# Block-sparse attention into a top-2 mixture of experts: a mask write moved ahead of the row maximum, the last batch's router logits moved behind an expert's second tile, scatters of one unit left unordered, and an exponential moved

## The chip, the cores and the metric

The kernel runs on one core of a Trainium2 chip. The metric is device time in microseconds (us), the median of the runs shown. TensorE (PE) multiplies matrices; VectorE (DVE), ScalarE (ACT) and GpSimd (POOL) do the other arithmetic; SyncE (SP) only issues DMAs. Each engine runs its own instructions in the order in which the program wrote them, and waits on semaphores for the others.

## The reference

Two parts, one behind the other. The attention, for 4 batches, 8 heads, 768 positions and a head size of 64:

```
scores = scale * q @ k.T                      # scale = 1/8
mask   = blocks of 32: neighbours, the first and last block, 3 sampled ones
scores = where(mask, scores, -1e9);  attn = exp(scores - max);  attn /= sum + 1e-9
out    = attn @ v
```

Its output, as x of 3072 tokens by 512, goes into eight experts:

```
noisy  = x @ w_gate + log1p(exp(x @ w_noise)) * noise
top2   = the two largest of 8;  top2_w = exp(top2_l - max) / (sum + 1e-9)
out[token] += top2_w * (relu(x[token] @ w1[e]) @ w2[e])     # 512 -> 1024 -> 512
```

## The kernel before, in words

**Attention** takes the first 380 us. A head has 6 tiles of 128 keys, so there are 192 steps. A step n computes exponentials of one tile of scores (`exp`, lines 290 to 304: PE writes `pe`, ACT writes `p`, in two halves), turns the 32-bit result into 16-bit pairs on DVE (`halve`, line 309), and multiplies the tile of three steps earlier with the values (`av`, line 335, 18 small matmuls into `po`). A head later in the program has its row maxima found meanwhile (`max_mm`, lines 251 and 252 on PE into `pm`, line 254 on ACT into `rl`; `max_red`, line 261 on DVE). When the six maxima of a head are there, `row_mm` (line 281) turns them into rows on PE, beside the `pm` of that step, and `row_put` (line 288, DVE) writes them into rows of `q2`, from which the exponentials subtract them. At the end of a head `av_end(.., "copy")` (line 347, ACT) copies `po` into `xo`, after which `po` may take the next head; DVE and POOL scale it. `Attention.steps` writes all this in one fixed order, and calls `background` between, which runs the router.

**Router.** `Router.run` is a generator, one for each batch of 768 tokens, and each `yield` is a place where it may pause. For the first three batches it runs in the gaps of the attention. For the last batch it pauses only at `MARK`, and `to_mark` (called from the expert loop) runs it to the next. It computes logits on PE (lines 586 and 588, from `r_xT`, the transposed tokens), copies them (line 595, `r_lc`), finds the two largest, computes the slot of each token (lines 677 to 717), and POOL scatters the token numbers and weights into the table `slots` in 12 indirect DMAs (line 723).

**Experts.** There are nine units. Unit 0 is expert 0 with 640 rows of the first three batches, unit 1 is expert 0's remaining 224 rows, units 2 to 8 are experts 1 to 7 with 816 rows. A unit has eight tiles of the first layer (`mm1`, line 892 on PE, line 897 on ACT and 898 on DVE: `hh` and `hl`, the high and low part) and up to seven chunks of 128 rows of the second layer (`mm2`, line 912). `finish` weights a chunk (line 940, DVE, `y`) and POOL scatters it into the output (line 942). Before that, POOL gathers what earlier units left there (line 858, `pv`). Weights arrive in 8 pieces an expert (line 797, SP) and are split into a high part (line 804, ACT) and a low part (line 805, DVE). Unit 0 starts while the last batch has yet to be routed. Unit 1 needs that routing: the slots, then the list `mt` (lines 814 and 818), the indices `gi` (line 827), the token rows `xg` (line 843, POOL) and their transpose `xtb` (line 853).

Of the kernel before, what the change touches and what calls it, by code (L numbers as in the profile page):

```python
# [44 lines left out]
class Attention:  # L45
# [271 lines left out]
    def later(self, steps, f):  # L317
        if steps:
            self.todo.setdefault(self.now + steps, []).append(f)
        else:  # L320
            f()
# [113 lines left out]
    def steps(self, on_group, background):  # L435
        NSTEP, LM, LA, GT = self.NSTEP, self.LM, self.LA, self.G * self.T
        for n in range(NSTEP + LA + 6 + self.ROWLATE):
            g, i = divmod(n, GT)
            self.now = n
            for f in self.todo.pop(n, []):  # L440
                f()
            for at, nm in self.LOADAT:
                if i == at and 4 <= g + 3 < self.NG:
                    self.load(g + 3, None, nm)
            for f, *a in self.plan.pop(n, []):
                f(*a)
            new = range(self.nmax, min(n + self.lead(n) + 1, self.T + self.XM + 1 + (n + 1) * self.RN // 4, NSTEP))
            self.nmax = max(self.nmax, new.stop)
            j = n - LA
            last = 0 <= j < NSTEP and j % self.T == self.T - 1  # L450
            if last:
                self.av(j)
            if n < NSTEP:
                self.exp(n, 0)
            self.av_end(j, "copy", on_group)
            slow = 1 if j < NSTEP - GT else 0
            self.av_end(j - 3 - slow, "high", on_group)
            if j == NSTEP - GT:
                self.av_end(j - 4, "high", on_group)
            self.age()  # L460
            for m in new:
                self.max_mm(m)
            self.row_mm()
            if n < NSTEP:
                self.exp(n, 1)
            if 0 <= j < NSTEP and not last:
                self.av(j)
            background(n, 0)
            self.av_end(j - 1, "sum", on_group)
            for m in new:  # L470
                self.max_red(m)
            if n < NSTEP:
                self.halve(n)
            self.row_put()
            background(n, 1)
            self.av_end(j - 1, "inverse", on_group)
            background(n, 2)
            self.av_end(j - 1, "scale", on_group)
            self.av_end(j - 4 - slow, "low", on_group)
            if j == NSTEP - GT:  # L480
                self.av_end(j - 5, "low", on_group)
            for at, part in self.VSPLITAT:
                if i == at and 2 < g + 2 < self.NG:
                    self.vsplit(g + 2, part)
            if i == self.DIFFAT and g + 2 < self.NG:
                self.diff(g + 2, slice(0, self.G))
            for at, part, h in self.CASTAT:
                if i == at and g + 3 < self.NG:
                    self.split(g + 3, part, h)
            for at, part in self.SPLITAT:  # L490
                if i == at and 0 < g < self.NG - 2:
                    self.split(g + 2, part)
            for at, part, h in self.FIRST:
                if g == 0 and i == at:
                    self.split(2, part, h)
            background(n, 3)


class Router:
# [73 lines left out]
    def run(self, b, ps):  # L573

        nc, T, D, pool = self.nc, self.T, self.D, self.pool
        KB = D // P
        last = b == self.B - 1
# [11 lines left out]
                                 stop=kb == KB - 1, skip_group_check=True)  # L589
        for _ in range(0 if last else self.HO):  # L590
            yield
        if last:
            yield self.MARK
        lc = tile([P, T, 32], F32, "lc")
        nc.vector.tensor_copy(lc, pv)
        yield
# [8 lines left out]
        u = tile([P, T, E], F32, "u")  # L605
# [51 lines left out]
        nc.vector.tensor_scalar(z0, ef, 0.0, None, op0=ALU.is_equal)  # L657
        yield
        yield self.MARK if last else None
        ex = tile([P, T], F32, "ex")  # L660
        nc.scalar.activation(ex, dl, AF.Exp)
        for _ in range(0 if last else self.YN):
            yield
        if last:
            yield self.MARK

        pp = ps()
        po = pp[:, 0:T * E].rearrange("p (t e) -> p t e", t=T)
# [51 lines left out]
        for t in range(T):  # L720
            for k in range(2):
                nc.gpsimd.memset(self.spacer, 0.0)
                s = nc.gpsimd.indirect_dma_start(
                    out=self.table, out_offset=bass.IndirectOffsetOnAxis(ap=sl[:, t, k:k + 1], axis=0),
                    in_=pi[:, t, k, :], in_offset=None)
# [7 lines left out]
class Experts:  # L733
# [200 lines left out]
    def finish(self, u, c, py):  # L934

        nc = self.nc
        r = self.st["u", u]
        m = self.rows_of(u, c)
        y = self.yp.tile([P, self.D], F32, name="y")
        nc.vector.scalar_tensor_tensor(y[0:m], py[0:m, 0:self.D], r["mt"].bitcast(F32)[0:m, c, 1:2], self.pv[0:m, c, :],  # L940
                                       op0=ALU.mult, op1=ALU.add)
        nc.gpsimd.indirect_dma_start(  # L942
            out=self.out, out_offset=bass.IndirectOffsetOnAxis(ap=r["mt"][0:m, c, 0:1], axis=0),
            in_=y[0:m], in_offset=None, bounds_check=self.N - 1, oob_is_err=False)


def overflow(tc, router, w1, w2, out, x_dram, table):
# [78 lines left out]
def kernel(ctx, tc, q, k, v, sampled_blocks, w_gate, w_noise, noise, w1, w2, out):  # L1026
    nc = tc.nc
# [8 lines left out]
    ex = Experts(tc, router, w1, w2, out, x_dram, table)  # L1036
# [18 lines left out]
    def to_mark():  # L1055
        while jobs:
            m = next(jobs[0], jobs)
            if m is jobs:
                jobs.pop(0)
            elif m == Router.MARK:  # L1060
                return
# [65 lines left out]
    for u in range(nu):  # L1127
# [5 lines left out]
        nn = nf + bool(nl)  # L1133
        for f in range(ex.FB):
            ex.mm1(u, f)
            to_mark()
            if u > 1 and f == 0 and nn:
                ex.meta(u + 1)
            if u == 0:
                for i in SPLITS[f]:  # L1140
                    ex.split_piece(0, i)
                    if i + 3 < 8:
                        ex.load_piece(0, i + 3)
            if u == 0 and f in (5, 6):

                ex.load_piece(1, f - 5)
            if u > 1 and nn and f >= 5:
                ex.load_piece(nxt, f - 5)
            if u == 2 and f == 0:
                ex.split_piece(e, 6)  # L1150
            if u > 1 and f == 1:
                ex.split_piece(e, 7)
            if u > 1 and f == 1 and nn:
                ex.indices(u + 1)
            if u > 1 and f < n:
                ex.paced(ex.gather_prev(u, ex.chunks(u)[f]))
            if u > 1 and 1 <= f <= nn:
                ex.paced(ex.gather(u + 1, f - 1))
            if u > 1 and 2 <= f <= nn:
                ex.xpose(u + 1, f - 2)  # L1160
# [59 lines left out]
```

## Time and profile before

| what | value |
|---|---|
| median of 3 runs | 954.87 us (949.98, 957.19, 954.87) |
| profiled execution | 961.59 us, of which the span is 959.8 us |
| mean granted clock of PE | 0.985 |
| busy: PE, DVE, ACT, POOL | 876.8, 526.2, 447.9, 353.2 us |
| attention, router of the first three batches | to about 382 us |
| unit 0 with the last batch's routing | 382 to 449.6 us |
| units 1 to 8 | 449.6 to 943 us |
| last scatter, overflow count | to 959.8 us |

The span is one execution on the core, and the 1.8 us between it and the time of that execution lie around it. The profiled execution is 6.7 us over the median. A window of the span says how long each engine was busy in it and at what granted clock, and a line of a timeline says what an instruction waited for ahead of it.

### The profile page before, as it was taken

The page shows a single profiled execution, that of the slowest core. Times are in us where ns is not written, and L with a number is a line of the kernel's source. Part 1 is how long each engine was busy: PE and PEld are TensorE (multiplying, and loading weights), DVE is VectorE, ACT ScalarE, POOL GpSimd, SP SyncE. Part 2 cuts the span into 40 slices and gives each one's busy share as a digit, 9 for nine tenths or more (in the row PEclk, how much of TensorE's full clock was granted, in tenths as well). Part 3 has the DMA queues.
Part 4 walks back from the last instruction along what each step waited for, and adds up shares of the span by engine and source line. Part 5 has one row for each costly group of instructions (what it writes and reads, how often), then busy time and mean ns, then how long its engine had stood idle before and what let it go on. Part 6 is the DMA issues. An engine that isn't in the chain of part 4 may idle for free.

```text
span 959.8 us, 21119 instructions
## 1 busy us (share of the span) xinstructions
PE 876.8 (91%) x8494; PEld 529.3 (55%) x8494; DVE 526.2 (55%) x1245; ACT 447.9 (47%) x973; POOL 353.2 (37%) x392
## 2 busy tenths in 40 slices
PE   6899998898899878798999999999999999999993
PEld 3566675566566546554655554554554554555541
DVE  7888889898989966452334323333333333333210
ACT  6989988898888755331322122222231231231200
POOL 5432232662364163265252342332432432523220
PEclk9999999999999989899999999999999999999997
DMA  7677776796779249548788296295493692782110
GB/s 206 140 180 191 189 155 155 155 183 171 155 161 177 57 80 181 157 79 205 192 184 211 92 225 174 73 230 165 113 246 111 142 235 91 180 211 83 55 43 29
DMA packets 206477, 145.56 MB, mean 152 GB/s; under 512 B 142182, under 2 KB 183271, under 8 KB 206370
## 3 DMA queue, kind: packets, MB, share of 16 engines
q1 hardware_dynamic: 173936, 80.07, 40.0%
q0 software_dynamic: 14256, 39.58, 13.7%
q10 hardware_dynamic: 18178, 24.48, 9.9%
q8 instruction: 68, 1.11, 0.5%
q14 instruction: 39, 0.32, 0.1%
HBM read 79.55 MB, written 26.32 MB: 110 GB/s over the span
## 4 chain that ended last, share of the span: by engine, by line
PE 47%; DMA 3%; issue 1%; POOL 1%; DVE 1%; SPq 0%; ACT 0%; POOLq 0%; ACTq 0%
PE ph L892 23%; PE py L912 22%; PE py L921 2%; DMA pv<-out_dram,gi 1%; DMA out_dram<-y,mt 1%; DMA xg<-x_rows,gi 1%; DVE y L940 1%; DMA xtb<-xg 1%; POOL xg L843 1%; DMA slots<-r_pay,r_sl 0%; DMA mt<-slots 0%; POOL pv L858 0%; SPq L853 0%; POOL out_dram L942 0%; DVE hl L898 0%
## 5 line engine op out<-in xcount | busy, mean ns | idle before, releaser
L304 ACT ACTIVATE p<-pe 128x384 int32<-128x384 f32 x384 | 193.3, 530 | 44.6 <-PE pe L303 25.7
L897 ACT ACTIVATE hh<-ph 128x408 f16<-128x408 f32 (+2 forms) x136 | 66.8, 492 | 269.8 <-PE ph L892 209.7
L898 DVE SCALAR_TENSOR_TENSOR hl<-ph,hh 128x408 f16<-128x408 f32 (+2 forms) x136 | 76.0, 560 | 172.7 <-ACT hh L897 159.6
L942 POOL DMA_INDIRECT out_dram<-y,mt x56 | 74.9, 1337 | 216.3 <-DVE y L940 105.2
L335 PEld LDWEIGHTS <-p 128*128 128x128 f16 x3456 | 127.4, 98 | 24.4 <-issue 1.7
L301 PE MATMUL pe<-q,k 128*128 128x384 f16 x384 | 127.2, 331 | 10.3 <-ACT p L304 5.4
L309 DVE TENSOR_SCALAR p<-p 128x1536 f16<-128x1536 uint16 x192 | 125.9, 656 | 7.4 <-ACT p L304 7.0
L303 PE MATMUL pe<-q,k 102*128 102x384 f16 x384 | 127.2, 331 | 0.9 <-DVE q L288 0.9
L912 PEld LDWEIGHTS <-hh 128*128 128x128 f16 x768 | 74.8, 98 | 95.5 <-issue 9.9
L261 DVE CUSTOM_DVE_ANT_0 rl<-pm,rl 128x384 f32<-128x384 f32 x192 | 106.1, 554 | 36.9 <-ACT rl L254 27.5
L335 PE MATMUL po<-vb,p 128*128 128x65 f16 x1152 | 122.2, 194 | 0.7 <-issue 0.7
L335 PE MATMUL po<-vx,p 128*128 128x65 f16 x1152 | 122.3, 195 | 0.5 <-DVE p L309 0.4
L940 DVE SCALAR_TENSOR_TENSOR y<-py,mt,pv 128x512 f32<-128x512 f32 (+2 forms) x56 | 41.2, 748 | 147.5 <-PE py L912 140.8
L335 PE MATMUL po<-vl,p 128*128 128x64 f16 x1152 | 122.0, 193 | 0.0
L892 PE MATMUL ph<-xta,w1hb 128*128 128x408 f16 x512 | 109.3, 336 | 0.0
L254 ACT ACTIVATE rl<-pm 128x384 f32<-128x384 f32 x192 | 100.2, 523 | 14.3 <-PE pm L252 13.2
L251 PE MATMUL pm<-k,q 88*128 88x384 f16 x192 | 65.4, 341 | 30.2 <-DVE q L288 21.6
L892 PE MATMUL ph<-xtb,w1ha 128*128 128x408 f16 (+1 forms) x448 | 91.2, 325 | 0.5 <-DMA xtb<-xg 0.5
L858 POOL DMA_INDIRECT pv<-out_dram,gi x56 | 56.8, 1014 | 94.2 <-ACT hh L897 65.6
L912 PE MATMUL py<-w2ha,hh 128*128 128x512 f16 x192 | 73.3, 382 | 4.6 <-DVE y L940 4.6
L892 PEld LDWEIGHTS <-w1ha 128*128 128x128 f16 x576 | 56.5, 99 | 36.0 <-DMA xtb<-xg 1.0
L224 POOL TENSOR_TENSOR kn<-raw_k,kn 128x384 f16<-128x384 f32 (+1 forms) x29 | 28.8, 993 | 124.8 <-ACT kn L222 103.6
(200 smaller groups left out, 1625.2 us busy)
## 6 DMA issues: line engine op xcount, KB each, us to landing
wraw<-in_moe_w_dram SPq DMA_DIRECT2D x60, 512.0 KB
raw_v<-in_v_dram ACTq DMA_DIRECT2D x16, 384.0 KB
out_dram<-zero ACTq DMA_DIRECT2D x24, 256.0 KB
x_rows<-x SPq DMA_DIRECT2D x16, 384.0 KB
raw_k<-in_k_dram ACTq DMA_DIRECT2D x12, 384.0 KB
raw_q<-in_q_dram ACTq DMA_DIRECT2D x12, 384.0 KB
k<-k SPq DMA_DIRECT2D x15, 192.0 KB
q<-q SPq DMA_DIRECT2D x15, 192.0 KB
```

The lines of the kernel that those rows point to most:

```text
L254: self.nc.scalar.activation(rl, pm[:, 1, 0:384], AF.Relu)
L261: self.nc.vector.tensor_tensor_reduce(rl, pm[:, 0, 0:384], rl, 1.0 / 64.0, -3.0e38, ALU.add, ALU.max, accum_out=mn[:, self.MR + t:self.MR ...
L301: nc.tensor.matmul(pe[:, 0:384], r["k1"][:, h, c, :], r["q1"][:, h, t, :], start=True, stop=False)
L303: nc.tensor.matmul(pe[:, 0:384], r["k2"][0:K, h, c, :], r["q2"][0:K, h, t, :], start=False, stop=True)
L304: nc.scalar.activation(p32[:, t].rearrange("p t c -> p (t c)"), pe[:, 0:384], AF.Exp, scale=0.125)
L309: self.nc.vector.tensor_scalar(p.rearrange("p t c w -> p (t c w)"), p32.bitcast(U16).rearrange("p t c -> p (t c)"), HC, None, op0=ALU.mult)
L335: self.nc.tensor.matmul(o, p[:, t, :, w], v, start=first and i == 0, stop=last and i == 2, skip_group_check=True)
L892: nc.tensor.matmul(ph[:, b, 0:m], w[wt][:, kb, fs], r["xt"][:, kb, a, o:o + m], start=i == 0, stop=i == last)
L897: self.pace = nc.scalar.activation(hv, ph[:, b, 0:m], AF.Relu)
L898: nc.vector.scalar_tensor_tensor(self.hl[:, f, o:o + m], ph[:, b, 0:m], 0.0, hv, op0=ALU.max, op1=ALU.subtract)
L912: nc.tensor.matmul(py, h[:, f, o], w[x][:, f, :], start=i == 0, stop=i == last)
L942: nc.gpsimd.indirect_dma_start(out=self.out, out_offset=bass.IndirectOffsetOnAxis(ap=r["mt"][0:m, c, 0:1], axis=0), in_=y[0:m], in_offset= ...
```

## The change

Five edits, of which the last touches two places.

1. In `Attention.steps`, `row_put` stands ahead of `max_red` and `halve` of its step, no longer behind them.
2. In the same function `av_end(j, "copy")` stands behind `max_mm` and `row_mm`, no longer ahead of them.
3. In `Router.run`, the last batch does not pause between its logits and their copy. For the other batches the exponential of the gates (line 661) stands behind the pauses and not ahead of them.
4. In the expert loop the last batch's router is not run behind the first tile of the first layer, only behind the second and later ones, and there behind the split and load of the weight pieces.
5. The scatters of one unit into the output are declared independent of each other, since a token has one slot of an expert. The gathers of the next unit wait for all of them.

```diff
@@ Attention.steps
             if n < NSTEP:
                 self.exp(n, 0)
-            self.av_end(j, "copy", on_group)
...
             for m in new:
                 self.max_mm(m)
             self.row_mm()
+            self.av_end(j, "copy", on_group)
...
             self.av_end(j - 1, "sum", on_group)
+            self.row_put()
             for m in new:
                 self.max_red(m)
             if n < NSTEP:
                 self.halve(n)
-            self.row_put()
@@ Router.run
         for _ in range(0 if last else self.HO):
             yield
-        if last:
-            yield self.MARK
         lc = tile([P, T, 32], F32, "lc")
...
         yield self.MARK if last else None
+        for _ in range(0 if last else self.YN):
+            yield
         ex = tile([P, T], F32, "ex")
         nc.scalar.activation(ex, dl, AF.Exp)
-        for _ in range(0 if last else self.YN):
-            yield
-        if last:
-            yield self.MARK
+        yield self.MARK if last else None
@@ Experts.finish
-        nc.gpsimd.indirect_dma_start(
+        s = nc.gpsimd.indirect_dma_start(
             out=self.out, ...
+        done = r.setdefault("done", [])
+        for p in done:
+            self.tc.declare_no_dep(s.ins, p.ins, reason="a token has one slot of an expert")
+        done.append(s)
@@ the expert loop
             ex.mm1(u, f)
-            to_mark()
-            if u > 1 and f == 0 and nn:
-                ex.meta(u + 1)
             if u == 0:
                 for i in SPLITS[f]:
                     ex.split_piece(0, i)
                     if i + 3 < 8:
                         ex.load_piece(0, i + 3)
+            if f:
+                to_mark()
+            if u > 1 and f == 0 and nn:
+                ex.meta(u + 1)
```

DVE at the end of a head, before:

```order
L261 ISA rl,mn_107<-pm,rl 128x384 [waits Activation_49]
L261 ISA mn_107 128x1
L309 TENSOR_SCALAR p_931<-p_914 128x1536 [waits Activation_49]
L350 TENSOR_SCALAR rc<-xo 128x6
L261 ISA rl,mn_107<-pm,rl 128x384 [waits DVE_49,Activation_49]
L261 ISA mn_107 128x1
L309 TENSOR_SCALAR p_972<-p_935 128x1536 [waits Activation_49]
L288 TENSOR_TENSOR q_101<-pm,ident 6x768
L352 RECIPROCAL rc<-rc 128x6 [waits DVE_49]
```

and now:

```order
L261 ISA rl,mn_107<-pm,rl 128x384 [waits Activation_49]
L261 ISA mn_107 128x1
L309 TENSOR_SCALAR p_931<-p_914 128x1536 [waits Activation_49]
L350 TENSOR_SCALAR rc<-xo 128x6
L288 TENSOR_TENSOR q_101<-pm,ident 6x768 [waits Activation_49]
L261 ISA rl,mn_107<-pm,rl 128x384 [waits DVE_49]
L261 ISA mn_107 128x1
L309 TENSOR_SCALAR p_973<-p_935 128x1536 [waits Activation_49]
L352 RECIPROCAL rc<-rc 128x6 [waits DVE_49]
```

The write of the mask rows (line 288) passes one reduction and one halving, and takes over the reduction's wait for ACT.

ACT at the same place, before:

```order
L304 ACTIVATE p_914<-pe 128x384 [waits DVE_49,PE_49]
L347 ACTIVATE xo<-po 128x390
L254 ACTIVATE rl<-pm 128x384 [waits PE_49]
L304 ACTIVATE p_914<-pe 128x384 [waits PE_49]
L304 ACTIVATE p_935<-pe 128x384 [waits DVE_49,PE_49]
```

and now:

```order
L304 ACTIVATE p_914<-pe 128x384 [waits DVE_49,PE_49]
L254 ACTIVATE rl<-pm 128x384 [waits PE_49]
L347 ACTIVATE xo<-po 128x390
L304 ACTIVATE p_914<-pe 128x384 [waits PE_49]
L304 ACTIVATE p_935<-pe 128x384 [waits DVE_49,PE_49]
```

The copy that frees `po` stands behind the `rl` of the first of the two steps; nothing else moved.

DVE in unit 0, where the last batch's logits are copied, before:

```order
L805 SCALAR_TENSOR_TENSOR w1la<-wraw,w1ha 128x4x256 [waits DMAHW2_49,Activation_49]
L805 SCALAR_TENSOR_TENSOR w1la<-wraw,w1ha 128x4x256 [waits DMAHW5_49,Activation_49]
L898 SCALAR_TENSOR_TENSOR hl<-ph,hh 128x320 [waits Activation_49] x2
L595 COPY r_lc<-py 128x192
L598 TENSOR_TENSOR r_lg<-r_lc 128x96 [waits DVE_49]
```

and now (the line numbers of the changed kernel are 2 or 3 lower):

```order
L802 SCALAR_TENSOR_TENSOR w1la<-wraw,w1ha 128x4x256 [waits DMAHW2_49,Activation_49]
L802 SCALAR_TENSOR_TENSOR w1la<-wraw,w1ha 128x4x256 [waits DMAHW5_49,Activation_49]
L895 SCALAR_TENSOR_TENSOR hl<-ph,hh 128x320 [waits Activation_49] x2
L802 SCALAR_TENSOR_TENSOR w1la<-wraw,w1ha 128x4x256 [waits DMAHW7_49,Activation_49]
L593 COPY r_lc<-py 128x192 [waits PE_49]
L596 TENSOR_TENSOR r_lg<-r_lc 128x96 [waits DVE_49]
```

On DVE the third split (of piece 3) stands ahead of the copy; on PE all 24 matmuls of a second tile stand ahead of the logits.

POOL, the last scatter of the slots, the first two scatters of unit 0's output and the first gather of unit 1's rows, before:

```order
L723 DMA slots<-r_pay,r_sl 28160x2 [waits DMASW1_49]
L942 DMA out_dram<-y,mt 3072x512 [waits DMAHW5_49,DMASW2_49,DVE_49]
L942 DMA out_dram<-y,mt 3072x512 [waits DMASW3_49,DMASW2_49,DVE_49]
L843 DMA xg<-x_rows,gi 128x1024 [waits DMAHW0_49,DMAHW6_49,DMASW4_49,DVE_49]
L843 DMA xg<-x_rows,gi 96x1024 [waits DMAHW1_49,DMASW5_49,DVE_49]
```

and now:

```order
L720 DMA slots<-r_pay,r_sl 28160x2 [waits DMASW1_49]
L939 DMA out_dram<-y,mt 3072x512 [waits DMAHW5_49,DMASW2_49,DVE_49]
L939 DMA out_dram<-y,mt 3072x512 [waits DMASW3_49,DVE_49]
L840 DMA xg<-x_rows,gi 128x1024 [waits DMAHW0_49,DMAHW6_49,DMASW4_49,DVE_49]
L840 DMA xg<-x_rows,gi 96x1024 [waits DMAHW1_49,DMASW5_49,DVE_49]
```

The second scatter no longer waits for DMASW2, the semaphore that the first one raises; the order of the rows is the same.

## Rows read from the trace of the kernel before

**Rows 1.** Windows: length; PE, PEld, DVE, ACT, POOL busy; clock, DMA share, GB/s.

```profile
37.00:315.00 278.00, 248.94 (x3836) 177.00 (x3833) 250.07 (x688) 242.50 (x595) 109.49 (x132) 1.00 0.76 169
384.00:408.00 24.00, 18.52 (x167) 13.04 (x166) 11.55 (x45) 7.86 (x16) 6.92 (x7) 0.86 0.53 157
```

**Rows 2.** Waits of PE, 37 to 315 us: us in total, times, longest.

```profile
PE pm L251 <- DVE q L288: 20.4, 22, 2.0
```

**Rows 3.** Waits of ACT, the same stretch.

```profile
ACT p L304 <- PE pe L303: 18.5, 30, 2.1
```

**Rows 4.** Timeline, DVE at one head's end: start, us, engine, line, idle before.

```profile
103.45 0.56 DVE L261 CUSTOM_DVE_ANT_0 rl<-pm,rl 128x384 f32<-128x384 f32 x1 [0.86 <-ACT rl L254]
104.59 0.56 DVE L261 CUSTOM_DVE_ANT_0 rl<-pm,rl 128x384 f32<-128x384 f32 x1
105.07 0.55 DVE L309 TENSOR_SCALAR p<-p 128x1536 f16<-128x1536 uint16 x1
105.66 0.96 DVE L288 TENSOR_TENSOR q<-pm,ident 6x768 f16<-6x768 f32 x1
```

**Rows 5.** Timeline, ACT at that head's end and one gap behind it.

```profile
102.50 0.54 ACT L347 ACTIVATE xo<-po 128x390 f32<-128x390 f32 x1
102.87 0.55 ACT L254 ACTIVATE rl<-pm 128x384 f32<-128x384 f32 x1
103.98 0.57 ACT L254 ACTIVATE rl<-pm 128x384 f32<-128x384 f32 x1
112.03 0.49 ACT L304 ACTIVATE p<-pe 128x384 int32<-128x384 f32 x1 [0.38 <-PE pe L303]
```

**Rows 6.** Timeline, PE at that head's end.

```profile
103.09 0.19 PE L335 MATMUL po<-vx,p 128*128 128x65 f16 x1
106.68 0.34 PE L251 MATMUL pm<-k,q 88*128 88x384 f16 x1 [0.81 <-DVE q L288]
```

**Rows 7.** Timeline, POOL products at this head and a later one.

```profile
105.48 0.91 POOL L224 TENSOR_TENSOR qn<-raw_q,qn 128x384 f16<-128x384 f32 x1 [2.12 <-ACT qn L222]
147.96 0.91 POOL L224 TENSOR_TENSOR qn<-raw_q,qn 128x384 f16<-128x384 f32 x1 [2.16 <-ACT qn L222]
```

**Rows 8.** Timeline, DVE at that later head.

```profile
148.04 1.25 DVE L309 TENSOR_SCALAR p<-p 128x1536 f16<-128x1536 uint16 x1
```

**Rows 9.** Timeline, PE in units 0 and 1.

```profile
390.50 0.21 PE L586 MATMUL py<-r_whl,r_xT 128*128 128x32 f16 x1 [4.87 <-DMA r_xT<-x]
442.14 0.38 PE L912 MATMUL py<-w2ha,hh 128*128 128x512 f16 x1 [3.41 <-DVE y L940]
449.63 0.37 PE L892 MATMUL ph<-xtb,w1ha 128*128 128x224 f16 x2 [0.46 <-DMA xtb<-xg]
```

**Rows 10.** Timeline, DVE in unit 0.

```profile
387.99 2.36 DVE L805 SCALAR_TENSOR_TENSOR w1la<-wraw,w1ha 128x1024 f16<-128x1024 f32 x2 [0.45 <-ACT w1ha L804]
398.67 0.35 DVE L595 COPY r_lc<-py 128x192 f32<-128x192 f32 x1
403.91 1.22 DVE L805 SCALAR_TENSOR_TENSOR w1la<-wraw,w1ha 128x1024 f16<-128x1024 f32 x1
409.61 0.24 DVE L677 TENSOR_TENSOR r_A<-r_A,py 128x96 f32<-128x96 f32 x1
440.20 1.23 DVE L805 SCALAR_TENSOR_TENSOR w1lb<-wraw,w1hb 128x1024 f16<-128x1024 f32 x1 [2.90 <-issue]
```

**Rows 11.** Timeline, POOL: first slot scatter, second scatter of the output.

```profile
411.80 1.02 POOL L723 DMA_INDIRECT slots<-r_pay,r_sl  x1 [19.02 <-DVE r_ot L715]
434.97 0.99 POOL L942 DMA_INDIRECT out_dram<-y,mt  x1 [4.42 <-DMA mt<-slots]
```

**Rows 12.** Chain of waits, two pieces ahead of unit 1: start, us, what.

```profile
432.75 2.19 DMA mt<-slots
...
436.27 6.36 DMA xg<-x_rows,gi
```

**Rows 13.** Timeline, ACT: the gates' exponential of the third batch.

```profile
324.80 0.21 ACT L661 ACTIVATE r_ex<-r_dl 128x6 f32<-128x6 f32 x1 [2.68 <-DVE r_dl L639]
```

## The prediction

> **What bounds the kernel now.** I read the stretches first (windows), then each engine's waits in the attention, then one head row by row, then the chain of waits and the timelines between 384 and 450 us. The windows show that the attention from 37 to 315 us has no single bound: of 278.0 us PE is busy 248.94, DVE 250.07 and ACT 242.50 [rows 1]. Three engines at 87 to 90% mean that small stalls pass from one to the next. PE's largest stall there is a matmul of a later head's maxima (line 251) that waits for the mask write on DVE (line 288): 20.4 us in 22 waits, 0.93 each [rows 2]. ACT's largest is for PE's scores: 18.5 us in 30 waits [rows 3]. These are largely the same stalls, seen one engine further on, so they must not be added.
>
> The second place is unit 0. PE waits 4.87 us for the transposed tokens [rows 9] and the clock of that stretch falls to 0.86 [rows 1]. The route to unit 1 then runs: logits copied at 398.67, slots multiplied out at 409.61 [rows 10], first slot scatter at 411.80 [rows 11], lists in `mt` [rows 12], rows gathered [rows 12], transposed, and unit 1's first matmul at 449.63, which waits a last 0.46 us for them [rows 9]. What is gained on that route, PE gains whole, since everything behind it is PE work.
>
> **Attention, edits 1 and 2.** In one head, DVE does reduction (103.45), halving, sum, reduction (104.59), halving (105.07), mask write (105.66 to 106.62), and PE's matmul starts at 106.68 [rows 4, 6]. With the write ahead, it still waits for the second `rl`, which ACT ends at 104.55 (103.98 + 0.57) [rows 5]. So it can run from about 104.58 to 105.54. The buffer `pm` is also read by the reduction of that step, which now follows, 0.56 long [rows 4]: free at about 106.13 where it was 106.62, so 0.5 us of the 0.81 wait goes [rows 6]. The halving ends about 1 us later; its values are multiplied three steps on, and a step takes 1.9 us (192 steps from 24 to 382 us), so there is cover.
>
> ACT's copy of `po` starts 0.37 later, one pitch of ACT (102.50 to 102.87 [rows 5]). PE's first `av` of the next head came at 103.09, when the copy had ended at 103.04 [rows 5, 6], so it now waits some 0.3 us. I find so little slack (0.05 us) in 14 of 31 heads, 0.3 to 0.9 in the others. That delay falls ahead of the wait for the mask write and eats what is left of it, so the two don't add: the head's stall goes from 0.93 to 0.3 or 0.4.
>
> What is this worth? PE's view gives 0.5 x 22 = 11 us, ACT's gives its gap behind a stall, 0.38 [rows 5], x 22 = 8.4. ACT is as busy as PE, so I take the smaller, rounded to **8 us**. The bounds: nothing, if other waits take the place; and 20.4, the whole wait [rows 2].
>
> **The exponential of the gates, edit 3.** ACT stands 2.68 us at 324.80 for DVE's `r_dl` [rows 13]. Two steps later its input is ready. But DVE is busy all through that stretch with the router and remains so; what ACT gains, it then waits for DVE. I take 0.4 us, one gap of ACT as in [rows 5]; bounds 0 and 2.7. The other two batches show no such wait, so nothing.
>
> **Logits behind the second tile, edits 3 and 4.** PE has the 3.3 us of the second tile as cover for the 4.87 of waiting [rows 9]; tokens still land at 390.50, so the logits end at about 391.6 as before. What delayed the copy was not this: DVE had `hl` of the second tile in front of the copy at 398.67 [rows 10]. Now the second tile is over by 388.6. DVE finishes the double split at 387.99 + 2.36 = 390.35 [rows 10], the two `hl` parts at 391.8, waits for ACT's high part of piece 3 until 392.3, splits its low part (1.22 [rows 10]) and copies the logits at about 393.5: 5.2 us earlier. Behind the router's first part stand the same two tiles and two splits as before (pieces 4 and 5 for 3 and 4), 5.7 us from there to the multiplication. With ACT's order a little less favourable I get 404.85 for 409.61, **4.8 us** earlier. The 12 slot scatters, their landing and `mt` keep their lengths, so `mt` and the loads on SP behind it move by 4.8.
>
> **Free scatters, edit 5.** The second scatter, issued at 434.97 [rows 11], had its `y` ready at 429.15 and waited for the first scatter's landing; the gathers of unit 1 stood behind it on POOL until 436.27 [rows 12]. Now they wait for `gi` alone, computed when `mt` lands (432.75 + 2.19 = 434.94 for its last part [rows 12], the first index at 434.41). That takes another 1.3 to 1.6 from the gathers, so the transposed rows come 6.3 earlier. PE can't use all of it: its last chunk of unit 0 starts at 442.14, having waited for a `y` [rows 9], which stood on DVE behind the split at 440.20, whose piece SP loads behind `mt` [rows 10]. That moves by 4.8. The chunk then runs 7.0 us to 449.17, and the 0.46 behind it disappears [rows 9]. Unit 1 starts 4.8 + 0.46 = **5.2 us** earlier. Bounds: 2, if a load or scatter queues anew, and 6.3. Later units wait for `y` or nothing, not for scatters; there I count 0, hidden by the 24 us units of PE work.
>
> PE's clock: it fell to half behind the 4.87 us wait (0.86 over the stretch [rows 1]). The wait now is 390.50 - 388.6 = 1.9 us, and may leave the clock up. The route is paced by DVE here, so I count nothing for it either way.
>
> **Sum.** 8 + 0.4 + 5.2 = 13.6 us. The profiled execution would go from 961.6 to 948.0; it stands 6.7 over the median. From the median 954.9 I predict **941.3 us**.
>
> **A rule that speaks against it.** The halving now stands later, where POOL works. At 148.04 a halving took 1.25 us where it takes 0.55 elsewhere [rows 4, 8], with a POOL product of 0.91 begun 0.08 us before it [rows 7]. In the head above, the product starts at 105.48, behind the halving at 105.07 [rows 4, 7]; now the halving would come at about 106.1 and meet it. In 14 heads such a product starts within 0.35 us of the mask write. The price is 0.3 to 0.7 us each on DVE, 4 to 10 us in all, which takes half of the attention's gain or all of it: 945 to 950. The Trainium skill states in "SBUF — State Buffer" (Who interferes with whom) that VectorE and GpSimd share a port pair as an exclusive lock, and that whichever starts second blocks for the other's whole instruction. The trace agrees in the one row of 1.25 us; by that rule alone the time would be in the band just named.
>
> **Rivals.**
> - *The attention gains nothing.* Either the halving meets POOL as said, or ACT, 87% busy, sets the pace. For it: three engines are near their limit [rows 1]. Against: the stall is in 22 heads and ACT's gap follows it [rows 2, 5]. Time 954.9 - 5.6 = 949.3.
> - *The whole wait goes.* If the buffer is not what PE waits for but the written rows, the result is there 1.1 us earlier and nearly all of 20.4 us can go on PE [rows 2]; with ACT following, 15 to 20 us. Time 931.
> - *Slower: the copy behind the `rl`.* PE can't start a head's `av` before `po` is copied; ACT's queue is full at this place, so each of 31 heads loses 0.37 us [rows 5], 11.5 us, and if nothing is gained on the mask write (the stall there is set by ACT's second `rl`), this decides. With 5.2 back in unit 0: 954.9 + 11.5 - 5.2 = 961.2. It decides if PE's first `av` waits for the copy in most heads and the write's wait stays over 0.8. Against: the slack in over half of the heads.
> - *Unit 0 gains only 2.* A new wait on DVE or for a piece of weights: 944.5, within the range.
>
> **Chances.** Forecast (with the last rival) 0.55, attention nothing 0.26, whole wait 0.12, slower 0.07. About 1% is what a measurement of this kernel can tell from no change: under 945.3 is faster, over 964.4 slower. Of the forecast 0.46 lies under 945.3, with the 0.12 that is 0.58 faster. The slower rival's 961 lies mostly within 1%: 0.02 of its chance is over. Same: 0.38 and slower 0.04. The range from 932 to 951 leaves out half of the 931 case and the slow one and the edges.
>
> **What the profile after would show.** Right: the waits of line 251 on the mask write fall from 20.4 to under 10, the wait of ACT for scores to about 10; the attention ends near 374 instead of 382. The logits' copy about 5 us closer behind unit 0's start, the first slot scatter 25 us behind it and not 30, the second output scatter without a wait for the first; unit 1 62 us behind unit 0's start, not 67.5. Wrong: a new wait of `av` for the copy of `po` on ACT, halvings over 1 us beside each mask write, or a `mt` that moves while PE's last chunk does not.

## The result, and the profile after

The changed kernel takes 946.66 us (median of 16 runs, 941.88 to 952.45), the kernel before 954.88 us (16 runs, 949.98 to 963.27) on the same chip. The ratio is 0.9906, with a 95% interval from 0.9881 to 0.9930: about 9.0 us faster, between 6.7 and 11.4. The forecast was 941.3 us, 13.6 less. The direction was right and the time lies inside the range, but the sum was too large by half: its 13.6 us is beyond the interval. The range, 932 to 951, is 19 us wide, so that lying inside it says little of the single steps.

The profiled executions flatter the change. The span went from 959.8 to 940.1 us, 19.7 less, while the medians differ by 8.2; the one was 6.7 us over its median, the other 4.8 under it. What must be explained is 9 us, not 20, and the difference between the two executions is a question of its own (experiments 1 and 4).

The attention's window in the changed kernel (columns as in [rows 1]):

```profile
37.00:315.00 278.00, 257.47 (x3943) 180.76 (x3940) 256.78 (x711) 248.78 (x612) 109.12 (x134) 1.00 0.78 169
```

PE, DVE and ACT all do more in the same 278 us: 257.5, 256.8 and 248.8 us where [rows 1] had 248.9, 250.1 and 242.5. The waits of PE in that window:

```profile
PE pm L251 <- DVE mn L261: 15.1, 28, 1.6
PE pe L301 <- ACT p L304: 1.8, 4, 0.5
PE po L335 <- ACT xo L347: 1.0, 4, 0.3
```

and of ACT:

```profile
ACT p L304 <- PE pe L303: 13.5, 20, 1.0
```

The wait for the mask write [rows 2] is gone from the list; in its place PE waits for the reduction, which now stands last at the shared buffer, 28 times for 0.54 us. Before the change line 251 waited for a reduction too, in the same window:

```profile
PE pm L251 <- DVE mn L261: 3.7, 4, 1.4
```

So the two waits of line 251 together fell from 24.1 to 15.1 us: the stall shrank as the prediction said, though not to under 10. The copy of `po` that was moved back costs 1.0 us in all. ACT's wait for scores fell from 18.5 [rows 3] to 13.5 here, but it is 20.1 and 21.1 us in experiments 2 and 5, which have the same early mask write, so it says little. DVE around one mask write of the changed kernel (start, us, engine, line):

```profile
103.90 0.96 DVE L288 TENSOR_TENSOR q<-pm,ident 6x768 f16<-6x768 f32 x1
104.90 0.56 DVE L261 CUSTOM_DVE_ANT_0 rl<-pm,rl 128x384 f32<-128x384 f32 x1
...
105.38 0.74 DVE L309 TENSOR_SCALAR p<-p 128x1536 f16<-128x1536 uint16 x1
...
106.32 0.56 DVE L355 TENSOR_TENSOR xr<-xo,rc 128x384 f32<-128x384 f32 x1
...
107.28 0.80 DVE L309 TENSOR_SCALAR p<-p 128x1536 f16<-128x1536 uint16 x1
...
108.94 1.27 DVE L309 TENSOR_SCALAR p<-p 128x1536 f16<-128x1536 uint16 x1
```

and POOL beside it:

```profile
104.80 0.91 POOL L224 TENSOR_TENSOR qn<-raw_q,qn 128x384 f16<-128x384 f32 x1 [2.11 <-ACT qn L222]
106.36 1.30 POOL L224 TENSOR_TENSOR qn<-raw_q,qn 128x384 f16<-128x384 f32 x1 [0.65 <-ACT qn L222]
108.68 1.12 POOL L364 TENSOR_TENSOR x<-xr,x 128x384 f16<-128x384 f32 x1 [1.02 <-ACT x L362]
```

The order is the one announced (write, reduction, halving), and each of the three halvings that follow began while POOL ran an instruction with two operands (two products of q, then the low part of x, line 364): 0.74, 0.80 and 1.27 us instead of the 0.55 of [rows 4]. Each ends 0.41 or 0.42 us behind the end of POOL's instruction. That is regular: of the 620 halvings in the fourteen profiles of this document that begin while POOL runs such an instruction, 616 end 0.41 to 0.46 us behind it.

The distance from one mask write to the next shows what that does. The next two mask writes before the change, and in the changed kernel:

```profile
115.54 0.96 DVE L288 TENSOR_TENSOR q<-pm,ident 6x768 f16<-6x768 f32 x1
126.05 0.96 DVE L288 TENSOR_TENSOR q<-pm,ident 6x768 f16<-6x768 f32 x1
```

```profile
113.80 0.96 DVE L288 TENSOR_TENSOR q<-pm,ident 6x768 f16<-6x768 f32 x1
123.84 0.96 DVE L288 TENSOR_TENSOR q<-pm,ident 6x768 f16<-6x768 f32 x1
```

The distance repeats to 0.03 us between executions wherever nothing odd happens:

| from the mask write at | before | changed |
|---|---|---|
| 105.66 / 103.90 (POOL's products of q beside it) | 9.88 | 9.90 |
| 115.54 / 113.80 (no such products) | 10.51 | 10.04 |

Of these two heads one gained 0.47 us, the other nothing. (Products of k begin some 5 us behind the mask write of the second, in both kernels.)

In unit 0 (PE, changed kernel):

```profile
368.76 0.98 PE L889 MATMUL ph<-xta,w1ha 128*128 128x320 f16 x3 [1.84 <-DMA xta<-xg]
423.57 0.59 PE L909 MATMUL py<-w2ha,hh 128*128 128x512 f16 x1 [2.92 <-DVE y L937]
430.05 0.35 PE L889 MATMUL ph<-xtb,w1ha 128*128 128x224 f16 x2
```

DVE:

```profile
352.04 0.17 DVE L824 TENSOR_SCALAR gi<-mt 128x5 int32<-128x5 int32 x1 [3.30 <-DMA mt<-slots]
381.29 0.35 DVE L593 COPY r_lc<-py 128x192 f32<-128x192 f32 x1
392.68 0.25 DVE L674 TENSOR_TENSOR r_A<-r_A,py 128x96 f32<-128x96 f32 x1
```

POOL:

```profile
394.87 1.02 POOL L720 DMA_INDIRECT slots<-r_pay,r_sl  x1 [18.45 <-DVE r_ot L712]
...
413.26 0.99 POOL L939 DMA_INDIRECT out_dram<-y,mt  x1 [0.31 <-issue]
417.53 1.05 POOL L840 DMA_INDIRECT xg<-x_rows,gi  x1 [3.27 <-DMA mt<-slots]
```

The 4.87 us wait for the last batch's tokens [rows 9] is not there, the second output scatter no longer waits ([rows 11] had 4.42), and the gather waits for `mt` alone. But there are two waits that the trace before did not have: DVE for the list of unit 0 (3.30 us, in the attention), and PE for unit 0's own rows `xta` (1.84 us, just behind its start at 366.62). Unit 1 starts 63.4 us behind unit 0, where it was 67.6 and 62 had been forecast.

### The profile page after: what moved, and what is told of

The parts are those of the page before. It is cut to its first block, busy times and chain, and to the rows that moved or that the text cites. A ratio compares the mean times of both kernels' runs of the same rounds, so it can differ in the third digit from the quotient of the medians.

```text
span 940.1 us, 21082 instructions
## 1 busy us (share of the span) xinstructions
PE 873.6 (93%) x8494; PEld 526.4 (56%) x8494; DVE 528.0 (56%) x1245; ACT 447.9 (48%) x973; POOL 363.2 (39%) x392
## 4 chain that ended last, share of the span: by engine, by line
PE 57%; DVE 21%; ACT 8%; DMA 5%; POOL 4%; issue 3%; SPq 0%; ACTq 0%; POOLq 0%; DVEq 0%
PE ph L889 26%; PE py L909 25%; DVE p L309 5%; DVE rl L261 5%; ACT p L304 3%; POOL slots L720 3%; DVE q L288 3%; PE py L918 2%; ACT rl L254 2%; DVE xr L355 1%; PE po L335 1%; DMA q<-q 1%; DVE vl L201 1%; DMA q<-qn 1%; ACT xo L347 1%
## 5 line engine op out<-in xcount | busy, mean ns | idle before, releaser
L304 ACT ACTIVATE p<-pe 128x384 int32<-128x384 f32 x384 | 195.6, 533 | 32.5 <-PE pe L303 20.9
L939 POOL DMA_INDIRECT out_dram<-y,mt x56 | 86.6, 1547 | 175.3 <-DVE y L937 163.9
L309 DVE TENSOR_SCALAR p<-p 128x1536 f16<-128x1536 uint16 x192 | 133.5, 696 | 5.8 <-ACT p L304 5.4
L251 PE MATMUL pm<-k,q 88*128 88x384 f16 x192 | 65.1, 339 | 22.9 <-DVE mn L261 21.1
```

The source lines that it names most:

```text
L304: nc.scalar.activation(p32[:, t].rearrange("p t c -> p (t c)"), pe[:, 0:384], AF.Exp, scale=0.125)
L309: self.nc.vector.tensor_scalar(p.rearrange("p t c w -> p (t c w)"), p32.bitcast(U16).rearrange("p t c -> p (t c)"), HC, None, op0=ALU.mult)
L939: s = nc.gpsimd.indirect_dma_start(out=self.out, out_offset=bass.IndirectOffsetOnAxis(ap=r["mt"][0:m, c, 0:1], axis=0), in_=y[0:m], in_off ...
```

## The experiments

Two theories were told apart first. A: unit 0's start depends on the routing of the third batch, so that a faster attention meets a wait for `xta`, and odd stalls decide whether it is seen. B: the profile before was typical, and the steps of the prediction add up. From experiment 5 on, A and B are the two theories that each expectation names for itself. Below, "u1" is the start of unit 1 behind the start of unit 0.

**1. The kernel before once more.** No edit.

> The kernel before, unchanged, for a second profile. Theory A (the start of unit 0 is set by the routing of the third batch, and the 12 us of odd stalls of PE and ACT between 335 and 375 us in the first profile are an event of that execution): the stalls are absent, the attention's last matmul comes near 369 us, PE then waits for the transposed rows of unit 0 (xta) until about 373 to 376, and the span is near 950. Theory B (the stalls belong to the kernel): they are there again at the same places, the first tile of unit 0 starts near 382, no wait for xta, span near 960.

973.47 us (971.6 of span), on a chip where that kernel's median is 967.93. A's picture of a stall that belongs to one execution was wrong: ACT stands again for 4.73 us, from 346 us on, and u1 is 67.50. But PE also waits 0.83 us for `xta`, so that wait was never far.

**2. Attention alone.** Edits 1 and 2.

```diff
-            self.av_end(j, "copy", on_group)
...
             self.row_mm()
+            self.av_end(j, "copy", on_group)
...
+            self.row_put()
             for m in new:
                 self.max_red(m)
             if n < NSTEP:
                 self.halve(n)
-            self.row_put()
```

> Edits 1 and 2 alone: mask write ahead of the reduction, copy of po behind the relu. Prediction's step: 8 us faster than before, all of it reaching the end. Theory A: the mask write of the 28th head comes 7 to 8.5 us earlier and the third batch's slots move by as much, so the gain reaches unit 0's start, 6 to 8 us, but PE waits 2 us or more for xta. Theory B: about 8 without such a wait. Rival (ACT sets the pace): under 3 us at the 28th head.

Ratio 0.9935 (0.9908 to 0.9961): 6.3 us of the 967.9, between 3.8 and 8.9. The distances are 9.90 and 10.04. The 28th mask write comes 291.4 us behind the first, where it was 304.0 in experiment 1 and 296.0 in the first profile, so the gain at the 28th head is 4.6 or 12.6 us, by the profile that it is held against. No wait for `xta`; so the 6 to 8 us of A and the mechanism of B, without A's wait.

**3. Unit 0 alone.** Edits 3, 4 and 5 with the attention's loop as before.

```diff
+            self.av_end(j, "copy", on_group)
...
             self.row_mm()
-            self.av_end(j, "copy", on_group)
...
-            self.row_put()
             for m in new:
                 self.max_red(m)
             if n < NSTEP:
                 self.halve(n)
+            self.row_put()
```

(against the changed kernel)

> Edits 3, 4 and 5 alone: gates' exponential later, logits behind the second tile, free scatters; the attention's loop as before. Prediction's step: 5.6 us faster. Theory A: from the end of the first tile of unit 0 to unit 1's first matmul 7.5 us are gained against the first profile of before, but in an execution where PE waits for xta the transposed tokens land under that wait, the 4.87 us wait of before shrinks too, and the time gains only 1 to 4 us. Theory B: 5 us or more.

Ratio 0.9961 (0.9936 to 0.9985): 3.8 us, between 1.5 and 6.2. In the profile, unit 0 runs as forecast: logits copied 11.39 us behind its start (16.60 before, 11.4 forecast), slots multiplied at 22.79 (27.54; 22.8), first slot scatter at 24.99 (29.73; 25), u1 61.62. The interval admits both theories.

**4. The changed kernel once more.** No edit.

> The changed kernel, unchanged, for a second profile. Theory A: PE again waits 1 to 3 us for xta in the first tile of unit 0, DVE 2 to 4 us for the list mt of unit 0, unit 1 starts 56.8 us behind the end of the first tile, within 0.5. Theory B: the wait for xta comes and goes with the odd stalls.

PE in unit 0 and unit 1 of this execution:

```profile
389.41 0.19 PE L586 MATMUL py<-r_whl,r_xT 128*128 128x32 f16 x1 [1.64 <-DMA r_xT<-x]
441.55 0.36 PE L889 MATMUL ph<-xtb,w1ha 128*128 128x224 f16 x2 [0.95 <-DMA xtb<-xg]
```

and ACT at the end of the attention:

```profile
339.38 0.49 ACT L304 ACTIVATE p<-pe 128x384 int32<-128x384 f32 x1 [5.99 <-remote]
```

Here ACT stands 5.99 us from 333 us on, there is no wait for `xta`, PE waits 1.64 us for the tokens (1.9 forecast), u1 is 60.60. In the first profile of the changed kernel the stall is absent and the two waits stand in its place. That is B's sentence on the wait that comes and goes, and it fits A's cause for it.

**5. The mask write alone.** Edit 1 only.

```diff
+            self.row_put()
             for m in new:
                 self.max_red(m)
             if n < NSTEP:
                 self.halve(n)
-            self.row_put()
```

> Edit 1 alone: the mask write ahead of the reduction, the copy of po where it was. Between two mask writes lie 9.88 us in heads with POOL's products of q at the mask write and 10.50 in the others before the change; 9.90 and 10.04 in the changed kernel. Theory A (the write alone does it): 9.9 and 10.05 here, 5 to 7 us faster. Theory B (the copy behind the relu is half of it, since the first reduction starts 0.37 us earlier): 10.3 or more in the second kind, under 4 us faster.

9.89 and 10.05; ratio 0.9943 (0.9909 to 0.9976), 5.5 us, between 2.3 and 8.8. The write alone gives the distances of experiment 2, and no other time as far as these intervals can tell.

**6. The copy alone.** Edit 2 only.

```diff
-            self.av_end(j, "copy", on_group)
...
             self.row_mm()
+            self.av_end(j, "copy", on_group)
```

> Edit 2 alone: the copy of po behind the relu of its step, the mask write at its old place. Theory A: the distances between mask writes stay 9.88 and 10.50, within 0.1, PE waits for the copy for 0.2 to 0.4 us in some heads. Theory B: the second kind falls to 10.2 to 10.3. Rival of the prediction (the copy costs 0.37 in each head): both kinds 0.3 longer.

9.88 and 10.50; one time of 969.84 beside a median of 968.79. PE's waits:

```profile
PE pm L251 <- DVE q L288: 18.0, 22, 1.9
...
PE po L335 <- ACT xo L347: 3.1, 11, 0.3
```

PE now waits for the copy in 11 heads, 3.1 us, and the wait for the write is 18.0 instead of 20.4: the delay is taken from the stall behind it. So it neither helps nor costs in these heads, and the rival in which it costs 0.37 us a head falls; the single time is too little to read.

**7 and 8. Both kernels without POOL's products** of k and q from the fifth pair of heads on. Their low halves keep what an earlier pair left.

```diff
-            self.later(1 if self.now else 0,
-                       lambda: nc.gpsimd.tensor_sub(...
+            if g < 4:
+                self.later(1 if self.now else 0,
+                           lambda: nc.gpsimd.tensor_sub(...
```

> The changed kernel without POOL's products of k and q from the fifth pair of heads on (the low halves keep what an earlier pair left). Theory A (in the heads with products of q the halvings meet them on DVE, which takes back what the earlier write gives): the halvings are near 0.56 us throughout the heads, and the heads that took 9.90 us take 9.4 to 9.6. Theory B (PE or ACT is the bound there): still 9.8 to 9.9, though the halvings are short.

> The kernel before, with the same products left out. Theory A: 9.8 to 9.9 and 10.4 to 10.5 as with them, since its halvings met little (0.55 to 0.68 us), so that the gain of the changed order without products is 0.4 us or more in both kinds of heads. Theory B: it falls as much as the changed kernel does.

DVE at the same head of the changed kernel without products (all line numbers are one higher):

```profile
105.65 0.55 DVE L310 TENSOR_SCALAR p<-p 128x1536 f16<-128x1536 uint16 x1
...
107.36 0.56 DVE L310 TENSOR_SCALAR p<-p 128x1536 f16<-128x1536 uint16 x1
...
108.78 0.55 DVE L310 TENSOR_SCALAR p<-p 128x1536 f16<-128x1536 uint16 x1
```

These three halvings are back at 0.55 and 0.56. (The next one, at 109.72, takes 0.80 beside the low part of x.) The distances:

| | with products of q | without |
|---|---|---|
| before | 9.88 | 10.51 |
| before, products left out | 9.88 | 10.51 |
| changed | 9.90 | 10.04 |
| changed, products left out | 9.57 | 10.04 |

In this head the products cost the kernel before nothing and the changed kernel 0.33 us. In four more heads with products, where the distances repeat well enough to be read, they cost the changed kernel 0.25 to 0.32 us and the kernel before nothing. In the other heads that have them the distances without products are up to 1.3 us shorter and up to 3.3 longer, with odd stalls among them, so that no price can be read. Theory A holds in the heads that can be read: PE does not set their length, and DVE, whose halvings meet POOL's products, has 0.4 us of idle time left in the 9.90. Each kernel was timed once here (957.64 and 965.91 us), which is too little to read.

**9. ACT's casts earlier,** so that the products start earlier.

```diff
             self.av_end(j, "copy", on_group)
+            for at, part, h in self.CASTAT:
+                if i == at and g + 3 < self.NG:
+                    self.split(g + 3, part, h)
             if n < NSTEP:
                 self.exp(n, 1)
...
-            for at, part, h in self.CASTAT:
-                if i == at and g + 3 < self.NG:
-                    self.split(g + 3, part, h)
```

> The changed kernel with ACT's casts of k and q one exponential earlier in their steps, so that POOL's products start about 0.4 us earlier and the first one ends under the mask write and the reduction, ahead of the halving. Theory A (the halvings that meet products cost the gain): the heads with products of q go from 9.90 to 9.6 to 9.7, the mean halving falls below the 696 ns of the changed kernel, and the kernel is 3 to 5 us faster than the changed one (ratio to before near 0.987). Theory B (PE is the bound): 9.9 stays, ratio near 0.991.

A miss: these heads take 10.19, longer than both. DVE:

```profile
104.74 0.55 DVE L309 TENSOR_SCALAR p<-p 128x1536 f16<-128x1536 uint16 x1
...
105.50 1.17 DVE L355 TENSOR_TENSOR xr<-xo,rc 128x384 f32<-128x384 f32 x1
```

POOL:

```profile
105.34 0.92 POOL L224 TENSOR_TENSOR qn<-raw_q,qn 128x384 f16<-128x384 f32 x1 [0.65 <-ACT qn L222]
```

The halving is clean at 0.55, but now the scaling of line 355 (two operands in SBUF) begins 0.16 us behind the start of the second product, takes 1.17 us instead of 0.56, and ends 0.41 us behind that product. The collision moved to the next instruction. With the two halvings that became shorter DVE has 0.17 us more to do than in the changed kernel; the head is 0.29 longer. The casts now also stand ahead of an exponential on ACT, and what that costs was not separated. The ratio, 0.9891 (0.9861 to 0.9922), comes from a chip on which the changed kernel was not timed, and cannot be told from its 0.9906.

**10. The third batch's router one step earlier.**

```diff
-        for _ in range(0 if last else self.YN):
+        for _ in range(0 if last else self.YN - 6 * (b == self.B - 2)):
             yield
         ex = tile([P, T], F32, "ex")
```

> The changed kernel with 6 pauses fewer in the third batch's router, so that its slots are scattered one step (1.8 us) earlier. Theory A (in some executions unit 0's rows xta come late and take back what unit 0 gains): no wait for xta in the profile, unit 1 61 us behind unit 0's start, and 1 to 2 us faster than the changed kernel over many runs (ratio near 0.989). Theory B (the wait for xta is rare or covered): ratio as that of the changed kernel, 0.991.

Ratio 0.9864 (0.9836 to 0.9891), the lowest of all, and six times within 956.63 to 958.99. Its interval overlaps with that of the changed kernel (0.9881 to 0.9930), so it is not shown to be faster, and the changed kernel was not timed on this chip. The profile does not support A's reason: PE still waits 0.70 us for `xta`, and u1 is 63.27, because PE waits 2.63 us for `xtb` at unit 1.

**11. Both of the last two.**

> Both of the above. Theory A: the two gains add, 4 to 7 us faster than the changed kernel, ratio near 0.985. Theory B: 0.991.

Ratio 0.9879 (0.9851 to 0.9907), 10.18 and 10.05: nothing added.

**12. Edit 5 undone** in the changed kernel.

```diff
-        done = r.setdefault("done", [])
-        for p in done:
-            self.tc.declare_no_dep(s.ins, p.ins, reason="a token has one slot of an expert")
-        done.append(s)
```

> The changed kernel with edit 5 undone: the scatters of a unit wait for one another as before. Prediction's step (free scatters bring the gathers 1.3 to 1.6 us forward, of which PE can use about 0.5): the first gather of unit 1 comes 23 to 24.5 us behind the first slot scatter, where the changed kernel has 22.2 to 22.7, PE waits 1 to 3 us for the transposed rows xtb at unit 1, and the time is 0.5 to 1.5 us over the changed kernel's, which is less than these rounds can tell. Rival (free scatters also help the later units): 3 us or more slower.

POOL:

```profile
422.54 0.99 POOL L939 DMA_INDIRECT out_dram<-y,mt  x1 [4.99 <-DMA mt<-slots]
423.84 1.05 POOL L840 DMA_INDIRECT xg<-x_rows,gi  x1 [0.30 <-issue]
```

The second scatter waits again, and the first gather comes 24.7 us behind the first slot scatter (22.0 to 23.2 in the seven profiles with free scatters). PE waits 0.87 us for `xtb`, under the 1 to 3 expected. The ratio is 0.9880 (0.9846 to 0.9913), again on another chip, and no slower than the changed kernel's: free scatters are worth nothing that these runs can tell, and a difference of 0.5 to 1.5 us they cannot tell. This execution too has no long ACT stall near 340 us, and shows the same two waits. DVE:

```profile
354.44 0.17 DVE L824 TENSOR_SCALAR gi<-mt 128x5 int32<-128x5 int32 x1 [5.63 <-DMA mt<-slots]
```

PE:

```profile
372.78 0.58 PE L889 MATMUL ph<-xta,w1ha 128*128 128x320 f16 x3 [2.07 <-DMA xta<-xg]
```

## Why the prediction was right, and where its sum went

**The bound, and where a gain would land: right.** Both places named gave time, and each alone was timed faster: attention 6.3 us (3.8 to 8.9), unit 0 with the gates' exponential 3.8 us (1.5 to 6.2). They add up to 10.1, which agrees with the 9.0 measured together.

**The mask write, 8 us: mechanism right, size not excluded, but not the same in every head.** The write stands ahead, and PE waits for the reduction in its place, 9.0 us less in the window. Timed alone it gave 6.3 us (3.8 to 8.9). In the profiles the 28th mask write comes 287.5 us behind the first, where it came 296.0 behind it before: 8.5 us, with the odd stalls of both executions in it. To leave most of these out, take each of the 27 distances up to there at its shortest in the profiles with the order of before (the first, and experiments 1, 3 and 6), and at its shortest with the new order (the changed kernel, and experiments 2, 4, 5 and 12): the differences add up to 8.3. What failed is the even price, ACT's gap of 0.38 us for each of 22 heads. The differences are 0.47 us in seven heads, 0.11 or less in nine (among them the head of [rows 4]) and 0.85 to 1.2 in three, the first among them. That they add up to about 8 is in part luck.

What holds the head of [rows 4] at nothing stood in the prediction as "a rule that speaks against it" and was given to a rival, not to the forecast: 0.3 to 0.7 us in 14 heads, 4 to 10 us. Measured, the products cost 0.25 to 0.33 us in the five heads where it can be read (experiments 7 and 8). For all 14 that would be 3.5 to 4.6 us, an estimate from these five that no run shows. The Trainium skill's page "SBUF — State Buffer" (Who interferes with whom) says that VectorE and GpSimd share a port pair as an exclusive lock, and that a VectorE instruction with two inputs in SBUF contends with a GpSimd one that reads SBUF. The halvings of 0.74 to 1.27 us beside POOL's instructions agree with the first, and the scaling of 1.17 us in experiment 9 with the second.

**The copy behind the relu: right.** Its 0.3 us is taken from the wait that follows, so edit 2 is neutral in the heads that were read (experiment 6), and the slower rival was without ground.

**The gates' exponential, 0.4 us: right.** ACT has no wait there any more, against 2.68 us in [rows 13]. The distance between the 28th and the 29th mask write is 13.07 and 13.08 in the two profiles of the changed kernel, and 13.55 and 13.56 in experiments 2 and 5, which have the attention's edits without this one: 0.48. With the attention's order of before it is less, 13.65 in experiment 3 against 13.88 and 13.87. One gap of ACT was taken as the size without a row that showed it there, so the fit is in part luck.

**Logits behind the second tile: right to 0.1 us,** where nothing else intervened (experiment 3). The order on DVE was what delayed the copy, not PE's wait.

**Unit 1 5.2 us earlier: the term that looks too large.** Six profiles have unit 0 as before (the first, and experiments 1, 2, 5, 6 and 8), seven have edits 3 to 5 (the changed kernel, and experiments 3, 4, 7, 9, 10 and 11). Unit 1 starts 64.9 to 68.1 us behind unit 0 in the first group, 66.7 in the mean, and 60.6 to 66.3 in the second, 62.5 in the mean: 4.2 earlier. Unit 2 starts 84.1 to 88.5 us behind unit 0, and 80.4 to 88.1, in the mean 86.1 and 82.8: 3.2 to 3.3 earlier. So about 1.0 us is lost inside unit 1, which the prediction took as unchanged. The spread within the groups is such that 5.2 is not excluded, and neither does the timing of experiment 3 (3.8 us, 1.5 to 6.2) exclude 5.6.

The prediction named the last chunk of unit 0 as what keeps PE from using the whole route. Two other waits it did not count. First, unit 0's own rows: PE waits 1.84, 1.45 and 0.70 us for `xta` in three of those seven (the changed kernel, and experiments 7 and 10) and 2.07 in experiment 12. Where that wait is over 1 us the logits are copied 14.7 to 15.2 us behind unit 0's start, in the other four 11.4 to 11.6, and in experiment 10 12.2. That the shorter attention brings this wait is not shown: experiment 1 has it (0.83) with the attention of before, and experiment 2 has the shorter attention without it. Second, the rows of unit 1: the prediction said that the last 0.46 us would go. It went in two of the seven (the changed kernel and experiment 3); in the other five PE, which arrives earlier too, waits 0.47 to 2.63 us for `xtb`. In the six it waits 0 to 3.82, so this is no wait that the change brought. In the four profiles where it is over 2 us (experiments 1, 7, 9 and 10), unit 1 runs at a mean granted clock of 0.92 or 0.93, between the two levels of 1.2 and 2.4 GHz, and takes 20.4 to 21.8 us. In the others it runs at 1.00 and takes 19.0 to 19.8, but 20.8 in experiment 11, with a wait of 1.24 us for `hl` in it. Unit 1 as a window, PE before and in experiment 9:

```profile
449.63:468.63 19.00, 19.00 (x221) 16.15 (x221) 4.58 (x10) 5.40 (x11) 6.07 (x6) 1.00 1.19 252
```

```profile
442.24:463.09 20.85, 20.73 (x221) 17.17 (x222) 4.60 (x10) 5.46 (x11) 4.03 (x4) 0.92 0.99 228
```

The same 221 matmuls take 20.85 us at a granted clock of 0.92 instead of 19.00 at 1.00: 1.85 us more, behind a wait of 2.16. From the start of unit 2 to PE's last matmul it is 474.2 to 474.6 us in every profile, so the step that counted nothing for units 2 to 8 was right, though a unit is 67.6 us of PE work and not the 24 that it names.

**Free scatters: the gathers move about as worked out, and the time shows nothing** (experiment 12). The first gather comes 22.0 to 23.2 us behind the first slot scatter with free scatters, and 23.1 to 24.7 without: 1.5 us in the mean, where 1.3 to 1.6 had been worked out. The prediction let PE use about 0.5 us of it, which is less than these runs can tell.

**What stays open.** How much of the 4.6 us between forecast and result is attention and how much unit 0 is not settled by the timings: the intervals of each alone still hold 8 and 5.6. The profiles put the larger miss in unit 0 (3.3 of 5.2, against 8.3 of 8), but 8.3, 0.5 and 3.3 add up to 12.1, more than the 9.0 that were timed (6.7 to 11.4); where the rest is lost was not found. That the wait for `xta` comes from the third batch's slots was inferred from where DVE and PE wait. Moving its router one step earlier gave the lowest ratio, but not by a margin that shows, and not with the profile that was expected.

## What to carry to other kernels

When an instruction is moved, look at what the instructions behind it will meet on the other engines at their new time; a price that a row of the trace already shows, in a known number of places, belongs in the sum and not among the rivals. Before counting a gain on a route as PE's, ask which other data PE's next work waits for and when they land, because an earlier PE may find the next transfer late; in experiment 9 a wait of 2.16 us was followed by 1.85 us lost in a stretch at a lower granted clock. A stall repeated at fixed places is best measured by the distance between two instructions of the same kind, which here repeats to 0.03 us while whole runs scatter by 10. But such a distance speaks for its own head: here the heads gained from nothing to over 1 us, and only all of them together could be held against the sum.

## What the runs showed of the hardware that was not expected

ACT stands for 4.0 to 9.4 us ahead of an instruction that starts between 334 and 358 us in 12 of the 14 profiles (4.63 us ahead of 340.60 in the first profile, 5.99 in experiment 4, 9.00 in experiment 10). In ten of the 12 the profile names "remote" as the releaser of such a stall. The two without a stall ahead of the list of unit 0 are the changed kernel's first profile and experiment 12. From the 29th to the 30th mask write they take 10.66 and 10.65 us, the others 15.9 to 20.4. Such stalls may be part of the 10 us by which runs of one kernel scatter, and where they stand the wait for `xta` is absent in nine profiles and 0.70 to 1.45 us in three; their cause was not found.
